# Start order, three zero fills, the order of attention and the last addition in a kernel for adaLN, infini-attention and a SwiGLU FFN

## The chip, the cores and the metric

The kernel runs on one core of one Trainium2 chip. Its time is the device time of one execution in microseconds (us). The core's engines work side by side and each takes its instructions in order from its own queue: TensorE (PE; its weight loads are listed apart as PEld), VectorE (DVE), ScalarE (ACT), GpSimd (POOL), and SyncE (SP), whose queue issues most DMA transfers. Where an engine needs what another has made, its instruction waits on a semaphore, and all that stands behind it on that engine waits with it.

## The reference, cut to what matters

```python
def _A_ref(x, wq, wk, wv, wo, beta):            # S=2048, D=576, H=32, Dh=18, N=4 segments of L=512
    ...
    g = _sigmoid(beta).reshape(1, H, 1, 1)
    for s in range(N):
        qs, ks, vs = q[:, :, s], k[:, :, s], v[:, :, s]
        logits = jnp.einsum("bhqd,bhkd->bhqk", qs, ks) * scale + mask
        p = _softmax(logits, axis=-1)
        a_dot = jnp.einsum("bhqk,bhkd->bhqd", p, vs)
        pq = phi(qs)                              # t + 1 where t > 0, exp(t) elsewhere
        num = jnp.einsum("bhld,bhde->bhle", pq, M)
        den = jnp.einsum("bhld,bhd->bhl", pq, z)[..., None] + 1e-6
        o = g * (num / den) + (1.0 - g) * a_dot
        outs.append(o)
        pk = phi(ks)
        M = M + jnp.einsum("bhld,bhle->bhde", pk, vs)
        z = z + jnp.einsum("bhld->bhd", pk)
    ...
    return o @ wo

def _B_ref(x, w_gate, w_up, w_down):             # F=4608
    return (_silu(x @ w_gate) * (x @ w_up)) @ w_down

mod = (_silu(c) @ w_mod).reshape(c.shape[0], 6, 1, -1)
sa, ca, ga, sb, cb, gb = (mod[:, i] for i in range(6))
h = _layernorm(x, axis=-1) * (1 + ca) + sa
x = x + ga * _A_ref(h, wq, wk, wv, wo, beta)
h = _layernorm(x, axis=-1) * (1 + cb) + sb
x = x + gb * _B_ref(h, w_gate, w_up, w_down)
```

All data is float32. `mask` is -1e9 for keys behind the query and zero for the keys up to it. Scale and shift of each layernorm come out of a small product of `silu(c)` with `w_mod`.

## The kernel before, in words

Tokens lie on the 128 partitions in tiles of 128 (four rows of tiles, 0 to 3, make one segment), or are transposed on TensorE so that channels lie there, in groups of 128 channels called `kt` (the fifth has 64). Products that need float32 accuracy are made from pairs of `fp32r` numbers: a value is cast to a high part (`hh`, `wqkh`, `wvh`) and DVE subtracts that from the value for the low part (`hl`, `wqkl`, `wvl`); three products of such parts make one.

**Start (0 to 18 us of the profile).** SP loads `x[0]` in two halves and a part of `w_mod` in four pieces (`wm`). DVE makes statistics of each of the four rows of tiles (lines L263 to L265; the power -1/2 is on POOL, L266), and ACT normalises them (L438, with `nb` from L437). PE multiplies `wm` by the broadcast `sgb` (the silu of `c`) into `pr`, one group of products for each piece of channels `k` in the order 4, 0, 1, 2, 3 (L449); ACT copies `pr` to `row` (L459), adding one to the scale's half by `pbias` (two fills on POOL, L456 and L457); PE turns `row` into columns (`pcr`, L463), and DVE copies them to `colv`. The transposes of the normalised `x[0]` (`pt`, L276) are issued by `transpose_group` from a later function, `heads`, and the scheduler places them among the products of `pr`; a fourth one of each group is held behind the last product (`low["pr"]`). Transposes into `fill` (L454, L465) compute nothing that is used.

**Projections (18 to 235 us).** Evacuation of the transposes by ACT (`hh`, L283) and DVE (`hl`, L285), products with the q and k weights (`pp`, L554) and with the v weights (`pv`, L583), and the memory of each segment. The statistics of the segments behind the first are made for four rows at once: one power of 128x4 on POOL (L266), then four normalisations on DVE (L270).

**Attention (235 to 527 us).** The units `u` are pairs of a segment and four heads, 32 in all (`NU`). What is issued when is written out by hand in `ORDER`, one string for each unit. Of its tokens, `s` makes scores again for the exponential on ACT, `r` makes scores for the row maximum on DVE (of unit u+2; two adjacent ones of `s` and `r` share TensorE), `V` multiplies by v, `E` ends a unit's sums, `m` and `n` prepare the maximum, `c` and `d` are the two halves of combining a unit's attention with its memory part, `M` and `X` are the wo product, `y<n>` is a part of preparing the FFN's input, `U` loads a unit, and `<` and `>` shift a token to the unit before or after. `d` is `comb_b`: DVE makes reciprocals (L774) and multiplies (`tmp`, L781), and the product is added to the output tile `o` (L782), on POOL for all units but the last, whose addition is on DVE.

Three tiles `qe0` to `qe2` need zeros outside of what is loaded into them. `early()` fills them on POOL (L342, 128x1024 each) as soon as POOL comes to them.

**Behind attention.** PE transposes `o` of the last segment (`pto`, L819, and `ptr`, L802), multiplies by wo (530.7 to 550 us), and from 550 us on the FFN runs, in which each product of 2x2 blocks is made of seven block products; the sums of blocks of its input that this needs are made before (`ys` and others, L1209 and L1221 on POOL).

The order of instructions on each engine is that of the program's text, except that a scheduler moves instructions by its own estimates of when they can run; `tc.issue_after` holds an instruction behind another, and inside `tc.manual_schedule()` the text's order stands.

Of the kernel before, what the change touches and what calls it, by code (L numbers as in the profile page):

```python
# [7 lines left out]
F32 = mybir.dt.float32  # L8
# [91 lines left out]
def f32(ap):  # L100
    return ap.bitcast(F32)
# [3 lines left out]
def block(ctx: ExitStack, tc: tile.TileContext, x, wqk, wv, wo, beta, wgu, wd, c, w_mod, wm01, out):  # L105
# [136 lines left out]
    def p1_unit(u, b, ps, tag, bufs, jp, jb, load_e):  # L242
# [9 lines left out]
        for i in range(6 - 3 * u):  # L252
            yield
        mt_a(u, ps, tag, bufs)
        mt_b(u)

    def ln_stats(wk, xs, n):
        st = wk.tile([P, n, 2, 6], F32, tag=f"st{n}", name="st")
        mv = wk.tile([P, n, 2], F32, tag=f"mv{n}", name="mv")
# [1616 lines left out]
```

## Time and profile before

| | us |
|---|---|
| median of 3 runs (1815.52 to 1815.91) | 1815.66 |
| the profiled execution | 1815.06 |
| its span | 1813.3 |
| first product of `hh` with weights (`pp`) begins | 17.91 |
| first `pto` of the last segment's last columns begins | 530.72 |

The span goes from the first to the last instruction that the profile shows; the execution's time has 1.8 us around it. In the profile a row of a timeline names start, duration, engine, line, operation, output <- inputs and shape (several equal ones in a row are put together, with their count behind an x), and in brackets for how long the engine had been idle and which instruction released it. A row of waits names the waiting instruction and the one that released it, with total, times and the longest. A duration runs from an instruction's start to its end, with all that holds it up in between.

### The profile page before, as it was taken

The numbers are of one execution on the slowest core, as the hardware profiler recorded it, in microseconds if no ns is written. First come the engines' busy times: TensorE is split into PE (matmuls) and PEld (weight loads), VectorE is DVE, ScalarE is ACT, GpSimd is POOL, SyncE is SP. The second block draws the span as 40 slices with busy tenths as digits, with TensorE's granted clock in tenths as the row PEclk, the third lists the DMA queues.
The fourth block names the chain that finished last, engine by engine and source line by source line (L and its number), as shares of the span: only waits on it lengthen the run. The fifth ranks groups of instructions, "written<-read, shape, count | busy, mean of one in ns | idle before, by whom it ended". The sixth has DMA issues, their size and how long they took to land.

```text
span 1813.3 us, 31111 instructions
## 1 busy us (share of the span) xinstructions
PE 1789.0 (99%) x11061; PEld 1515.2 (84%) x11061; DVE 1480.0 (82%) x3277; ACT 949.5 (52%) x2073; POOL 490.9 (27%) x707
## 2 busy tenths in 40 slices
PE   8999999999989999999999999999999999999999
PEld 5888867767778888888888888888888888888888
DVE  7567589999968888889888898668888888888886
ACT  6444578778866445444544444434544544544542
POOL 3000146555660544544454444100000000000000
PEclk9999999999999999999999999999999999999999
DMA  8678766577678455555544543594324324323331
GB/s 287 234 239 281 236 195 180 165 195 214 179 238 269 160 185 175 164 172 188 190 144 140 174 155 121 193 293 138 107 79 130 107 80 130 107 81 129 107 103 53
DMA packets 178563, 304.51 MB, mean 168 GB/s; under 512 B 25304, under 2 KB 108184, under 8 KB 176616
## 3 DMA queue, kind: packets, MB, share of 16 engines
q1 hardware_dynamic: 151032, 248.66, 43.9%
q10 hardware_dynamic: 27376, 53.86, 8.5%
q8 instruction: 88, 1.44, 0.3%
q14 instruction: 67, 0.55, 0.1%
HBM read 188.42 MB, written 113.33 MB: 166 GB/s over the span
## 4 chain that ended last, share of the span: by engine, by line
PE 68%; DVE 2%; DMA 1%; POOL 1%; issue 1%; ACT 1%; ACTq 0%; DVEq 0%
PE A L1388 24%; PE pd L1516 13%; PE C L1388 12%; PE pd L1497 10%; PE B L1388 6%; PE pw L846 1%; DMA y<-yD 1%; DVE wr L1338 0%; DVE wl L1353 0%; DVE dl L1378 0%; PE pt L1288 0%; ACT Pt L725 0%; PE av L744 0%; POOL Pt L730 0%; DVE acc L1526 0%
## 5 line engine op out<-in xcount | busy, mean ns | idle before, releaser
L1388 PE MATMUL A<-y,wh 128*128 128x512 f32 x1152 | 406.1, 393 | 1.2 <-ACT B L1434 0.9
L1388 PEld LDWEIGHTS A<-y,wh 128*128 128x128 f32 x1152 | 216.6, 188 | 46.2 <-ACT B L1434 2.4
L1353 DVE TENSOR_TENSOR wl<-O,wh 128x256 fp32r<-128x256 f32 x504 | 248.0, 497 | 2.1 <-ACT wh L1352 1.6
L211 DVE CUSTOM_DVE_ANT_0 junk<-s,tri 128x384 bf16<-128x384 f32 (+3 forms) x512 | 218.6, 486 | 25.2 <-PE s L689 12.7
L1388 PE MATMUL A<-y,wl 128*128 128x512 f32 x576 | 226.9, 394 | 0.0
L1502 DVE TENSOR_TENSOR acc<-acc,pd 128x576 f32<-128x576 f32 x216 | 162.4, 752 | 59.0 <-PE pd L1497 51.5
L1388 PE MATMUL C<-y,wh 128*128 128x512 f32 x576 | 203.0, 393 | 0.5 <-DVE cu L1411 0.5
L1352 ACT CAST wh<-O 128x256 fp32r<-128x256 f32 x504 | 197.6, 405 | 1.5 <-DMA yD<-st 1.2
L1526 DVE TENSOR_TENSOR acc<-acc,pd 128x576 f32<-128x576 f32 x156 | 116.9, 750 | 89.7 <-PE pd L1516 89.3
L1516 PE MATMUL pd<-dh,ah 128*128 128x288 f32 x640 | 189.0, 295 | 0.5 <-DVE x L1520 0.5
L1516 PE MATMUL pd<-dh,al 128*128 128x288 f32 x640 | 189.1, 296 | 0.0
L1516 PE MATMUL pd<-dl,ah 128*128 128x288 f32 x640 | 188.8, 295 | 0.0
L1343 POOL TENSOR_TENSOR O<-O 128x384 f32<-128x384 f32 x132 | 149.1, 1144 | 139.0 <-DMA O<-in_wgu_dram 64.3
L1457 ACT CAST ah<-sg 128x512 fp32r<-128x512 f32 x192 | 119.2, 621 | 77.9 <-DVE sg L1412 71.4
L725 ACT ACTIVATE Pt<-s 128x512 f32<-128x512 f32 x256 | 136.0, 599 | 21.4 <-PE s L718 15.2
L1458 DVE TENSOR_TENSOR al<-sg,ah 128x512 fp32r<-128x512 f32 x192 | 136.4, 710 | 10.4 <-ACT ah L1457 10.2
L1497 PE MATMUL pd<-dh,ah 128*128 128x288 f32 x448 | 133.0, 297 | 0.0
L1497 PE MATMUL pd<-dh,al 128*128 128x288 f32 x448 | 132.5, 296 | 0.0
L1497 PE MATMUL pd<-dl,ah 128*128 128x288 f32 x448 | 132.3, 295 | 0.0
L1516 PEld LDWEIGHTS pd<-dl,ah 128*128 128x128 f32 x640 | 120.5, 188 | 7.2
L1516 PEld LDWEIGHTS pd<-dh,ah 128*128 128x128 f32 x640 | 120.8, 189 | 6.8 <-DVE x L1520 0.8
L1388 PEld LDWEIGHTS C<-y,wh 128*128 128x128 f32 x576 | 108.3, 188 | 21.5 <-DVE cu L1411 1.2
(412 smaller groups left out, 4336.6 us busy)
## 6 DMA issues: line engine op xcount, KB each, us to landing
O<-in_wgu_dram SPq DMA_DIRECT2D x36, 768.0 KB
O<-oD SPq DMA_DIRECT2D x36, 512.0 KB
oD<-O ACTq DMA_DIRECT2D x34, 512.0 KB
ks<-kD SPq DMA_DIRECT2D x64, 216.0 KB
qs<-qD SPq DMA_DIRECT2D x64, 216.0 KB
O<-in_wgu_dram SPq DMA_DIRECT2D x36, 384.0 KB
rD<-wr ACTq DMA_DIRECT2D x36, 336.0 KB
wr<-rD SPq DMA_DIRECT2D x35, 336.0 KB
```

Source lines behind the costliest of these rows:

```text
L211: nc.vector.tensor_tensor_reduce(junk[:, :n], bank[:, o:o + n], tri[:, L - n:], 1.0, -3e38, op0=ALU.add, op1=ALU.max, accum_out=mcol[u][0] ...
L725: nc.scalar.activation(pt[:, h], bank, AF.Exp, scale=SCALE)
L1343: eng.tensor_tensor(o[:, d], o[:, a], o[:, b], op=op)
L1352: nc.scalar.copy(wh, o)
L1353: later.append(lambda: nc.vector.tensor_tensor(wl, o, f32(wh), op=ALU.subtract))
L1388: nc.tensor.matmul(bank, lhsT=a, rhs=b, start=(first and n == 0), stop=(n == 6), skip_group_check=not first)
L1457: nc.scalar.copy(ah, src)
L1458: later.append(lambda: nc.vector.tensor_tensor(al, src, f32(ah), op=ALU.subtract))
L1497: nc.tensor.matmul(pd[:, i, :288], lhsT=a[:, tk], rhs=w, start=(k == 0), stop=(k == 2))
L1502: nc.vector.tensor_tensor(o, o, pd[:, :, :288], op=ALU.add)
L1516: nc.tensor.matmul(pd[:, i, :288], lhsT=a[:, tk], rhs=w, start=(k == 0), stop=(k == 5))
L1526: nc.vector.tensor_tensor(o, o, pd[:, :, :288], op=ALU.add)
```

## The change

It has four parts.

1. *Start.* The block is put under `tc.manual_schedule()`. `norm0` makes the statistics of two rows and then their `nb` and normalisation, first for rows 0 and 1, then for 2 and 3; the `sgb` copy stands ahead of both. The transposes of `kt` 0 to 3 are taken out of `heads` and put among the products of `pr` by hand (`tr0`, `pt0`); eight for rows 0 and 1 ahead of the products `k` = 1 and `k` = 2, the other eight behind the last product. The five `fill` transposes ahead of `row` go, and of the nine behind it six stay. `pbias` is filled behind the statistics.
2. *Zero fills.* The three fills of `qe` are held behind the power of the second statistics (`low["ln", 4]`, the first that is made for four rows).
3. *Order.* `ORDER` has new strings with the same tokens for the same units. Two lines of 33 are shown below.
4. *Additions.* The last unit's addition is shared: DVE adds the first three of four blocks of 72 columns, POOL the fourth, and `tmp` lies in a buffer of its own (`woraw`, not in use any more). The addition of unit 29 (`NU - 3`) goes from POOL to DVE.

```diff
-    "s s n s s V0123 <<d y75 y87 E y109 y105 y44 s s y122 y98 s s y111 y76 y129 >p s s",
-    "s s s M0 y99 M1 M2 M3 y100 X <<c >M0 y116 x y124 >M1 >M2 y117 y102 y89 >M3 >X <<d <c y112 y130 y53 s y131 s s s y113 s s s y115 y127 y128 V0123 E >V0123 >E <d y125 c d y118 >c y126 >d",
+    "s T y99 y116 s s y122 y127 s >M0 <<d >M1 y86 >M2 E y129 >M3 <c <d s >X y88 y53 y100 s s s s s",
+    "s s s y123 >M0 y110 y87 y117 >M1 >M2 y76 >M3 <c y118 s s y130 s y124 >X s s s y131 s y115 V0123 y111 y89 y128 <d E >V0123 c y112 y125 >E d >c y113 y126 >d",
...
-        nc.gpsimd.tensor_tensor(rs, rs, mhalf[:, :n], op=ALU.pow)
+        low.setdefault(("ln", n), nc.gpsimd.tensor_tensor(rs, rs, mhalf[:, :n], op=ALU.pow))
...
-                nc.gpsimd.memset(f32(q_[n]), 0.0)
+                with tc.issue_after(low["ln", 4].ins):
+                    nc.gpsimd.memset(f32(q_[n]), 0.0)
...
+            man.enter_context(tc.manual_schedule())
...
-            for i in range(4):
-                mv, rs = ln_stats(wk, [xs[0][:, i, :]], 1)
-                nb = wk.tile([P, 1], F32, tag="nb1", name="nb")
-                nc.vector.tensor_scalar(nb, mv[:, 0, 0:1], rs[:, 0:1], -1.0, op0=ALU.mult, op1=ALU.mult)
-                nc.scalar.activation(xs[0][:, i, :], xs[0][:, i, :], AF.Identity, scale=rs[:, 0:1], bias=nb[:, 0:1])
+            def norm0(ids):
+                ln = [ln_stats(wk, [xs[0][:, i, :]], 1) for i in ids]
+                for i, (mv, rs) in zip(ids, ln):
+                    nb = wk.tile([P, 1], F32, tag="nb1", name="nb")
+                    nc.vector.tensor_scalar(nb, mv[:, 0, 0:1], rs[:, 0:1], -1.0, op0=ALU.mult, op1=ALU.mult)
+                    nc.scalar.activation(xs[0][:, i, :], xs[0][:, i, :], AF.Identity, scale=rs[:, 0:1], bias=nb[:, 0:1])
 
             sgb = wk.tile([P, 5, 32], F32, tag="sgb", name="sgb", bufs=1)
             nc.vector.tensor_copy(sgb, sg.unsqueeze(2).to_broadcast([P, 5, 32]))
+            norm0((0, 1))
+            norm0((2, 3))
             pr = ps.tile([P, L], F32, tag="m", name="pr", bufs=1)
+            pt0 = [ps.tile([P, L], F32, tag="s1" if kt in (2, 3) else "t", name="pt", bufs=2) for kt in range(4)]
+
+            def tr0(ks, ids):
+                for kt in ks:
+                    for i in ids:
+                        nc.tensor.transpose(pt0[kt][:, 128 * i:128 * i + 128], xs[0][:, i, 128 * kt:128 * kt + 128], ident)
...
             for k in (4, 0, 1, 2, 3):
+                if k == 1:
+                    tr0((0, 1), (0, 1))
+                elif k == 2:
+                    tr0((2, 3), (0, 1))
...
-            for i in range(5):
-                nc.tensor.transpose(fill[:, i % 4, :], wm[:, 7, 112 * i:112 * i + 128], ident)
...
+            tr0((0, 1, 2), (2, 3))
...
-            for i in range(9):
+            tr0((3,), (2, 3))
+            for i in range(6):
...
-            tmp = wk.tile([P, 320], F32, tag="tmp", name="tmp")[:, :288].rearrange("p (i h z) -> p i h z", i=4, h=4)
+            last = u == NU - 1
+            tmp = (wk.tile([P, D], F32, tag="woraw", name="tmp", bufs=1) if last else
+                   wk.tile([P, 320], F32, tag="tmp", name="tmp"))[:, :288].rearrange("p (i h z) -> p i h z", i=4, h=4)
             nc.vector.tensor_tensor(tmp, v[:, :, :, :DH], rb, op=ALU.mult)
-            (nc.vector if u == NU - 1 else nc.gpsimd).tensor_tensor(dst, dst, tmp, op=ALU.add)
+            k = 3 if last else 4 if u == NU - 3 else 0
+            if k:
+                nc.vector.tensor_tensor(dst[:, :k], dst[:, :k], tmp[:, :k], op=ALU.add)
+            if k < 4:
+                nc.gpsimd.tensor_tensor(dst[:, k:], dst[:, k:], tmp[:, k:], op=ALU.add)
```

How the instructions stand at three places (engine queues in the order in which they are issued; in brackets whom a row waits for, a name with DMAHW being a transfer).

TensorE at the start, before: the groups of `pr` and, between them, transposes of the normalised `x[0]`.

```order
L449 MATMUL pr<-wm,sgb 32x320 [waits DMAHW4_49]
L449 MATMUL pr<-wm,sgb 32x320 x3
L276 MATMUL pt<-ident,x_265 128x128 [waits DMAHW1_49,Activation_49]
L276 MATMUL pt<-ident,x_265 128x128 x3
L276 MATMUL pt<-ident,x_265 128x128 [waits Activation_49]
L276 MATMUL pt<-ident,x_265 128x128 x2
L449 MATMUL pr<-wm,sgb 32x320 [waits DMAHW5_49]
L449 MATMUL pr<-wm,sgb 32x320 x3
L276 MATMUL pt<-ident,x_265 128x128 [waits DMAHW3_49,Activation_49]
L276 MATMUL pt<-ident,x_265 128x128 x4
L449 MATMUL pr<-wm,sgb 32x320 [waits DMAHW6_49]
```

The same place in the changed kernel, where L468 is the product of `pr` and L455 the transpose:

```order
L455 MATMUL pt<-ident,x_267 128x128 x2
L468 MATMUL pr<-wm,sgb 32x320 [waits DMAHW4_49]
L468 MATMUL pr<-wm,sgb 32x320 x3
L455 MATMUL pt<-ident,x_267 128x128 x4
L468 MATMUL pr<-wm,sgb 32x320 [waits DMAHW5_49]
L468 MATMUL pr<-wm,sgb 32x320 x3
L468 MATMUL pr<-wm,sgb 32x320 [waits DMAHW6_49]
L468 MATMUL pr<-wm,sgb 32x320 x3
L455 MATMUL pt<-ident,x_267 128x128 [waits DMAHW3_49,Activation_49]
L455 MATMUL pt<-ident,x_267 128x128 [waits Activation_49]
L455 MATMUL pt<-ident,x_267 128x128 x4
```

The transposes of rows 2 and 3 (the wait for DMAHW3) have moved from between the last two groups of `pr` to behind the last.

POOL between the first and the second statistics, before; `pk` and `vs` are small fills, `omc` a copy, and L266 is the power:

```order
L266 TENSOR_TENSOR rs<-rs,mhalf 128x1 [waits DVE_49] x2
L472 MEMSET pk 128x4x64 [waits DMAHW5_49,DMAHW4_49,DMAHW6_49,DMAHW2_49,PE_49]
L342 MEMSET qe 128x1024 x3
L601 COPY omc<-omg 18x8 [waits DVE_49]
L601 COPY omc<-omg 18x8 [waits Pool_49]
L601 COPY omc<-omg 18x8 x2
L266 TENSOR_TENSOR rs<-rs,mhalf 128x4 [waits DVE_49,Pool_49]
L578 MEMSET vs_2095 128x4x32 [waits DMAHW5_49,PE_49,Activation_49]
```

And in the changed kernel, with the power at L268 and the fills at L344:

```order
L491 MEMSET pk 128x4x64 [waits DMAHW4_49,DMAHW5_49,DMAHW2_49,DMAHW6_49,PE_49,Pool_49]
L623 COPY omc<-omg 18x8 [waits DVE_49]
L623 COPY omc<-omg 18x8 [waits Pool_49]
L623 COPY omc<-omg 18x8 x2
L268 TENSOR_TENSOR rs<-rs,mhalf 128x4 [waits DVE_49,Pool_49]
L344 MEMSET qe 128x1024 x3
L600 MEMSET vs_2090 128x4x32 [waits DMAHW5_49,PE_49,Activation_49]
```

The three fills have moved from ahead of the copies to directly behind the 128x4 power. On DVE the four normalisations that wait for this power are followed by `fl` and `wvl`, as before.

POOL at the end of attention, before; L1209 and L1221 are sums for the FFN's input, L782 the additions to `o`, L730 masks:

```order
L782 TENSOR_TENSOR o_6413<-o_6413,tmp 128x4x72 [waits DVE_49]
L730 AFFINE_SELECT Pt<-Pt 128x4x128 [waits Activation_49] x2
L730 AFFINE_SELECT Pt<-Pt 128x4x128
L730 AFFINE_SELECT Pt<-Pt 128x4x128 [waits Activation_49]
L1209 TENSOR_TENSOR yh_5571<-yh_5571,yh_5573 128x256
L1209 TENSOR_TENSOR yh_5571<-yh_5571 96x256
L1209 TENSOR_TENSOR yh_5571<-yh_5571,yh_5574 96x256 [waits Pool_49]
L782 TENSOR_TENSOR o_6413<-o_6413,tmp 128x4x72 [waits DVE_49] x2
L1221 TENSOR_TENSOR ys<-yh_5571,yh_5572 128x512 [waits PE_49]
L1221 TENSOR_TENSOR o_6413<-yh_5571,yh_5573 128x512
```

And in the changed kernel (L752 masks, L1237 and L1249 sums, L810 additions):

```order
L752 AFFINE_SELECT Pt<-Pt 128x4x128
L752 AFFINE_SELECT Pt<-Pt 128x4x128 [waits Activation_49]
L1237 TENSOR_TENSOR yh_5619<-yh_5619,yh_5621 128x256 [waits Pool_49]
L1237 TENSOR_TENSOR yh_5619<-yh_5619,yh_5622 96x256 x2
L810 TENSOR_TENSOR o_6396<-o_6396,tmp 128x4x72 [waits DVE_49]
L810 TENSOR_TENSOR o_6396<-o_6396,tmp 128x72 [waits DVE_49]
L1249 TENSOR_TENSOR ys<-yh_5619,yh_5620 128x512 [waits PE_49]
L1249 TENSOR_TENSOR o_6396<-yh_5619,yh_5621 128x512
```

Behind the last masks two full additions have become one, and the last unit's 72 columns stand directly ahead of the first L1249.

DVE at the same place, before: reciprocals (L774), multiplications (L781) and the last addition (L782), for the units 29, 30 and 31.

```order
L774 RECIPROCAL r_8393<-px 128x16 [waits PE_49]
L781 TENSOR_TENSOR tmp<-px,r_8393 128x288 [waits DVE_49]
L1119 TENSOR_TENSOR yo<-yh_5574,yo 32x256 [waits DMAHW7_49,Activation_49]
L774 RECIPROCAL r_8404<-px 128x16 [waits PE_49]
L781 TENSOR_TENSOR tmp<-px,r_8404 128x288 [waits DVE_49,Pool_49]
L774 RECIPROCAL r_8416<-px 128x16 [waits PE_49]
L781 TENSOR_TENSOR tmp<-px,r_8416 128x288 [waits DVE_49,Pool_49]
L782 TENSOR_TENSOR o_6413<-o_6413,tmp 128x4x72 [waits DVE_49]
```

And in the changed kernel (L796, L805, L808):

```order
L796 RECIPROCAL r_8366<-px 128x16 [waits PE_49]
L805 TENSOR_TENSOR tmp<-px,r_8366 128x288 [waits DVE_49,Pool_49]
L808 TENSOR_TENSOR o_6396<-o_6396,tmp 128x4x72 [waits DVE_49]
L1145 TENSOR_TENSOR yo<-yh_5621,yo 128x256 [waits Activation_49]
L1147 TENSOR_TENSOR yo<-yh_5622,yo 32x256 [waits DMAHW0_49]
L796 RECIPROCAL r_8399<-px 128x16 [waits PE_49]
L805 TENSOR_TENSOR tmp<-px,r_8399 128x288 [waits DVE_49]
L796 RECIPROCAL r_8411<-px 128x16 [waits PE_49]
L805 TENSOR_TENSOR tmp<-px,r_8411 128x288 [waits DMAHW6_49,DVE_49]
L808 TENSOR_TENSOR o_6396<-o_6396,tmp 128x3x72 [waits DVE_49]
```

Unit 29's addition stands on DVE behind its multiplication, and the last unit's multiplication no longer waits for POOL.

More of the change, by code (lines that the diff above doesn't have):

```diff
@@ L255, in p1_unit @@
         mt_b(u)
+    low = {}
     def ln_stats(wk, xs, n):
@@ L270, in xhat, with transpose_group @@
         nc.vector.tensor_scalar(dst, src, mv[:, i, 0:1], rs[:, i:i + 1], op0=ALU.subtract, op1=ALU.mult)
-    def transpose_group(pt, src, kt, behind=None):
+    def transpose_group(pt, src, kt):
         n = P if kt < 4 else 64
         for i in range(4):
-            with tc.issue_after(behind.ins) if behind and i == 3 else ExitStack():
-                nc.tensor.transpose(pt[:n, 128 * i:128 * i + 128], src(i)[:, 128 * kt:128 * kt + n], ident)
+            nc.tensor.transpose(pt[:n, 128 * i:128 * i + 128], src(i)[:, 128 * kt:128 * kt + n], ident)
     def evac_split(wk, pt, kt, hi, lo, sc, bi, tag="hf"):
@@ L377, in load_x @@
                 yield
-        rq, low = {}, {}
+        rq = {}
         def load_qk(t):
@@ L422, in block @@
             m0 = pool(p0, "m0")
+            man = ExitStack()
+            man.enter_context(tc.manual_schedule())
             gx = load_x(0)
@@ L451, in block @@
             low["pr"] = last
-            fill = ps.tile([P, 4, P], F32, tag="p", name="fill", bufs=3)
-            for i in range(5):
-                nc.tensor.transpose(fill[:, i % 4, :], wm[:, 7, 112 * i:112 * i + 128], ident)
             pbias = wk.tile([P, 1], F32, tag="pbias", name="pbias", bufs=1)
@@ L468, in block @@
             nc.vector.tensor_copy(colv[0:64, 4], pcv[0:64, 1, 2, :, 0])
+            man.close()
         pb = pool(p1, "pb", 2)
@@ L507, in trans_in @@
             for kt in range(5):
-                pt = ps.tile([P, L], F32, tag="s1" if s == 0 and kt in (2, 3) else "t", name="pt", bufs=2)
-                transpose_group(pt, lambda i: xs[s][:, i, :], kt, low["pr"] if s == 0 else None)
+                if s == 0 and kt < 4:
+                    pt = pt0[kt]
+                else:
+                    pt = ps.tile([P, L], F32, tag="t", name="pt", bufs=2)
+                    transpose_group(pt, lambda i: xs[s][:, i, :], kt)
                 if kt < 4:
```

1 line of the change is left out of this document (added), and 54 rows, old and new, of the table ORDER.

## The prediction

> **What bounds the kernel now.** I read the page first, then busy time by stage, then PE's waits, then the timeline at the places the diff touches. The page's busy time:
>
> ```profile
> span 1813.3 us, 31111 instructions
> PE 1789.0 (99%) x11061; PEld 1515.2 (84%) x11061; DVE 1480.0 (82%) x3277; ACT 949.5 (52%) x2073; POOL 490.9 (27%) x707
> ```
>
> PE is idle for only 24.3 us in all, so an edit can gain little unless it touches that idle time or the clock. By stage (start:end, length, then busy time and instructions of PE, PEld, DVE, ACT and POOL, then granted clock, DMA share, GB/s):
>
> ```profile
> 0.00:17.91 17.91, 9.95 (x73) 5.12 (x73) 7.69 (x30) 6.20 (x9) 10.10 (x35) 1.00 0.83 306
> 24.00:50.00 26.00, 25.87 (x124) 21.07 (x123) 22.28 (x46) 17.75 (x34) 2.66 (x5) 1.00 0.94 315
> 250.00:514.00 264.00, 260.60 (x2506) 187.27 (x2503) 240.26 (x1028) 207.45 (x427) 156.30 (x335) 1.00 0.65 186
> 529.00:560.00 31.00, 29.28 (x173) 27.26 (x174) 23.36 (x44) 17.19 (x37) 6.58 (x7) 0.89 0.99 332
> ```
>
> The first row is the start (8.0 us of PE idle). In the second PE has no slack, so a shift of the start is carried on whole. The third is steady attention: PE idle 3.4 us, DVE idle 23.7. The fourth has the clock at 0.89. PE's waits (total, times, longest) name the two single stalls:
>
> ```profile
> PE pr L449 <- DVE mv L264: 7.6, 1, 7.6
> PE pto L819 <- DVE o L782: 3.3, 1, 3.3
> ```
>
> The first is the wait for the first data; the second is the addition that the change shares out.
>
> **Term 1: the start.** The rows (start, duration, engine, line, operation; in brackets the idle time before it and its releaser):
>
> ```profile
> 8.95 1.54 DVE L263 BATCH_NORM_STATS2 st<-x 128x6 f32<-128x288 f32 x4 [1.29 <-DMA x<-in_x_dram]
> 10.41 0.32 DVE L437 TENSOR_SCALAR nb<-mv,rs 128x1 f32<-128x1 f32 x2
> ...
> 10.64 1.62 ACT L438 ACTIVATE x<-x,nb,rs 128x576 f32<-128x576 f32 x2 [7.97 <-DVE nb L437]
> 11.70 1.76 PE L276 MATMUL pt<-ident,x 128*128 128x128 f32 x7
> ...
> 13.39 0.89 PE L449 MATMUL pr<-wm,sgb 128*32 128x320 f32 x8
> 14.15 0.49 DVE L388 CAST wqkh<-wraw 128x640 fp32r<-128x640 f32 x1 [0.63 <-DMA wraw<-in_wqk_dram]
> 14.21 0.76 PE L276 MATMUL pt<-ident,x 128*128 128x128 f32 x5
> 14.90 0.75 PE L449 MATMUL pr<-wm,sgb 128*32 128x320 f32 x8
> 16.66 3.43 POOL L342 MEMSET qe<- 128x1024 f32 x3
> 17.03 2.17 DVE L388 CAST wqkh<-wraw 128x640 fp32r<-128x640 f32 x2
> 19.12 1.54 DVE L389 TENSOR_TENSOR wqkl<-wraw,wqkh 128x640 fp32r<-128x640 f32 x2
> 21.32 0.50 PE L554 MATMUL pp<-hl,wqkh 128*128 128x512 f32 x1
> ```
>
> Before, nb of rows 0 and 1 stood behind the four statistics of rows 2 and 3, which waited for their data until 8.95. Now it stands ahead of them, so both rows are normalised 1.5 us sooner or more (8.95 against 10.41) and their transposes leave the path. The five transposes (0.76) ahead of the last weight group go behind it: the column vector and the first casts come 0.8 us sooner, perhaps 1.2 with the gaps between. The two casts took 2.17 while the zero fills ran, against 0.49 for the one without: 2.17 - 2*0.49 = 1.2 more goes with the fills. In all 2.0 to 2.4 for DVE's chain of casts, differences and hl; I take 1.8, as ACT's hh and the third piece of weights can limit it too: **-1.8**, bounds -0.7 (the transposes alone) and -2.4. The sgb copy ahead of the statistics costs nothing: PE waits for weights there. The bias fills, now behind a pair of small powers on POOL, are needed only by the row. The fill transposes (14 before, 6 now) stood in PE's idle time and cost nothing.
>
> **Term 2: the fills at the second statistics.** The three fills now stand on POOL directly behind this power, and four DVE normalisations wait for the same power:
>
> ```profile
> 48.04 1.02 POOL L266 TENSOR_TENSOR rs<-rs,mhalf 128x4 f32<-128x4 f32 x1 [18.78 <-DVE rs L265]
> 49.09 2.05 DVE L270 TENSOR_SCALAR x<-x,mv,rs 128x576 f32<-128x576 f32 x4 [1.20 <-POOL rs L266]
> ...
> 51.66 0.75 DVE L112 TENSOR_TENSOR wvl<-wvraw,wvh 128x576 fp32r<-128x576 f32 x1
> 53.13 0.29 PE L583 MATMUL pv<-wvl,hr 128*128 128x288 f32 x1
> 17.88 1.32 DVE L388 CAST wqkh<-wraw 128x640 fp32r<-128x640 f32 x1
> ```
>
> The last row is the second cast under the fills: 1.32 - 0.49 = 0.83 of waiting behind one fill. A normalisation has the same form (one float32 SBUF input, 0.51 each), and the fills follow without a wait, so each of the three goes ahead of one: 3*0.83 = 2.5 late. Behind them on DVE stands wvl, which is done at 52.41 and read at 53.13, 0.72 before PE needs it; PE's queue is in order. The stall is 2.5 - 0.7 = **+1.8**. Bounds: 0 (the normalisations go first) and 3.43 - 0.72 = 2.7. DVE's own lag vanishes in later idle time, PE's doesn't. So terms 1 and 2 about cancel.
>
> **Term 3: the last addition.**
>
> ```profile
> 525.66 0.26 DVE L774 RECIPROCAL r<-px 128x16 f32<-128x16 f32 x1 [3.24 <-PE px L766]
> 526.28 1.54 POOL L782 TENSOR_TENSOR o<-o,tmp 128x288 f32<-128x288 f32 x2
> 527.10 0.46 DVE L781 TENSOR_TENSOR tmp<-px,r 128x288 f32<-128x288 f32 x1 [0.30 <-POOL o L782]
> 527.59 2.98 DVE L782 TENSOR_TENSOR o<-o,tmp 128x288 f32<-128x288 f32 x1
> 527.78 1.26 POOL L1221 TENSOR_TENSOR ys<-yh,yh 128x512 f32<-128x512 f32 x1
> 529.00 1.26 POOL L1221 TENSOR_TENSOR o<-yh,yh 128x512 f32<-128x512 f32 x1
> 530.72 0.45 PE L819 MATMUL pto<-ident,o 128*128 128x128 f32 x1 [3.27 <-DVE o L782]
> ```
>
> The DVE add of 288 columns is shown with 2.98, where the multiplication of 288 took 0.46. It ends at 530.57, just after POOL's second L1221 (530.26): it waited for both. Now tmp has its own buffer (no 0.30 wait: it ends at 527.26), unit 29's addition is off POOL, and DVE adds 216 columns (0.46*216/288 = 0.35) while POOL's 72 columns (at most a quarter to a half of 0.77, say 0.4) stand ahead of L1221. One after the other they end at 528.0; PE resumes at about 528.1 for 530.72. I take **-2.5**. If DVE's part loses the port to one L1221 it is -2.5 + 1.26 = -1.3, to both about -0.1; the best is -3.0 (both side by side). Unit 29's addition on DVE costs nothing: DVE idles 3.24 before 525.66; without that cover 0.4.
>
> The Trainium skill, "SBUF — State Buffer", section "SBUF: two separate sides", says that between a DVE operation with two SBUF inputs and a GpSimd one that reads SBUF, whichever starts first holds the shared port pair for its whole instruction, and the other fully blocks. By that rule the add would have waited for one operation at most. The 2.98 disagrees, so the measurement decides; by the rule term 3 is what I take, by the row it can still be lost to both.
>
> **Term 4: the clock.** Windows of 3.41 us, same columns:
>
> ```profile
> 518.92:522.33 3.41, 2.84 (x30) 1.38 (x32) 3.25 (x8) 2.84 (x7) 2.26 (x4) 1.00 0.66 222
> ...
> 525.74:529.16 3.42, 1.20 (x7) 0.78 (x7) 2.93 (x5) 0.05 (x1) 3.42 (x5) 1.00 0.95 319
> 529.16:532.57 3.41, 1.85 (x10) 1.74 (x10) 2.10 (x2) 1.10 (x2) 3.41 (x3) 0.50 1.01 405
> 532.57:535.98 3.41, 3.41 (x16) 3.41 (x15) 1.38 (x2) 1.69 (x4) 3.01 (x4) 0.50 1.02 339
> ```
>
> After a window with PE busy 1.20 of 3.42 the clock is halved for two windows; after one with 2.84 it isn't. PE works from 530.72 to 535.98 at half speed, 5.3 us, which costs half: 2.6. With the stall at 0.7 instead of 3.3, such a window holds some 2 to 2.5 us of work, nearer to 2.84 than to 1.20, so I take **-2.6**; the other end is 0.
>
> The Trainium skill, "TensorE: Matmul & The Clock Gate", Part 1, gives free-running windows of about 3.4 us and a drop after an idle one. The length agrees with these rows (two windows at 0.50); the drop here came after a window that was 35% busy, so idle need not mean empty. By the page's rule a window with 2 us of work keeps the clock, and rival 2 falls away.
>
> **Term 5: the order of attention.** The tokens are the same; 252 adjacent score pairs share TensorE instead of 254. No row shows what another order does. PE's idle 3.4 us bounds the gain; the loss has no bound but DVE, whose commonest work there is the row maximum:
>
> ```profile
> L211 DVE CUSTOM_DVE_ANT_0 junk<-s,tri 128x384 bf16<-128x384 f32 (+3 forms) x512 | 218.6, 486 | 25.2 <-PE s L689 12.7
> ```
>
> One such operation (486 ns) late in each of some 30 units would be +14.6. I take 0, nearer to the small bound, since 240 of 264 us of DVE work leaves 23.7 to absorb shifts.
>
> **Sum.** -1.8 + 1.8 - 2.5 - 2.6 + 0 = -5.1. The profiled execution took 1815.06 us (1.8 around its span), 0.6 below the median 1815.66. 1815.06 - 5.1 = 1810.0; against the median **1810.6 us**. A measurement of this kernel tells 0.2% (3.6 us) from no change.
>
> **Rivals.**
> 1. *The last addition loses the port again.* For it: the 2.98. Against: fewer POOL operations ahead. Then term 3 is -0.1 and term 4 is 0: 1815.66 - 0.1 = 1815.6, no change. Lost once, with the clock falling: -1.3, 1814.4, no change.
> 2. *The clock falls all the same,* after a shorter stall. Sum -2.5: 1813.2, no change.
> 3. *Slower: attention in the new order starves DVE.* Place: the waits of the row maximum on the scores, 12.7 us now. Price 486 ns a unit, +14.6 over 30 units: 1810.6 + 14.6 = 1825.2. It decides from 5.1 + 3.6 = 8.7 us, 0.29 us a unit. For it: DVE is 91% busy there, and nearly every line is reordered. Against: the slack of 23.7.
> 4. *The new order gains too,* up to PE's 3.4 us of idle: 1807.2, and a little more where it shortens the last units' run to the addition.
>
> **Chances.** The forecast 0.45; rival 1 lost twice 0.13; lost once 0.10 (half of it with the clock kept: -1.3 - 2.6 = -3.9, faster); rival 2 0.08; rival 3 0.15; rival 4 0.09. Faster: 0.45 + 0.05 + 0.09 = 0.59. Same: 0.13 + 0.05 + 0.08 = 0.26. Slower: 0.15. The range goes from 1804.3 (rival 4 with the best ends of terms 1 to 3: 1807.2 - 0.6 - 1.8 - 0.5) to 1817.6 (rival 1 with the weak ends of terms 1 and 2: 1815.6 + 1.1 + 0.9); outside lie rival 3 and a few hundredths below.
>
> **What would show it.** Term 1: two casts at 0.49 each and hl's first product near 19.5. Term 2: fills of some 3.4 us behind the 128x4 power, four normalisations taking about 4.5 instead of 2.05, and PE waiting for wvl. Term 3: the wait of pto on o at about 0.7, and a DVE addition of 216 columns well under 1 us. Term 4: a clock of 1.00 from 529 to 536. Term 5: DVE idle in attention near 24 us. The forecast is wrong if the addition again shows some 3 us, if the clock still falls, or if attention's length moves by more than 4 us.

## The result, and the profile after

The changed kernel takes 1809.41 us (median of 8 runs, 1807.21 to 1813.06) for 1815.51 us of the kernel before beside it (8 runs, 1813.69 to 1815.91). The ratio is 0.997, with a 95% interval of 0.9960 to 0.9979: 6.1 us less by the medians. The profiled execution took 1810.5 us (4.6 less than that of before) with a span of 1808.8. Single executions of one kernel lie 2 to 4 us to either side of its median, some further, so places are compared by profiles and totals by medians; a profile shows one execution alone.

The page of the changed kernel:

```profile
span 1808.8 us, 31104 instructions
PE 1783.9 (99%) x11053; PEld 1512.5 (84%) x11053; DVE 1485.3 (82%) x3278; ACT 947.8 (52%) x2073; POOL 493.5 (27%) x707
```

PE's idle time did not shrink: 24.9 us now, 24.3 before. Its busy time fell by 5.1 us. Its waits (total, times, longest) say that the stall at the last addition is gone and that others have come:

```profile
PE pr L468 <- DVE mv L266: 7.8, 1, 7.8
PE pw L874 <- DVE xr L879: 2.4, 1, 2.4
PE C L1416 <- DVE cu L1439: 1.5, 1, 1.5
PE pv L605 <- DVE wvl L112: 1.4, 1, 1.4
PE A L1416 <- DMA y<-yD: 1.4, 1, 1.4
PE pto L847 <- DVE tmp L805: 0.9, 1, 0.9
```

The timeline of the changed kernel, first at the start and at the second statistics, then at the last addition:

```profile
16.24 0.88 DVE L390 CAST wqkh<-wraw 128x640 fp32r<-128x640 f32 x2
19.25 0.50 PE L576 MATMUL pp<-hl,wqkh 128*128 128x512 f32 x1
...
46.77 2.75 POOL L344 MEMSET qe<- 128x1024 f32 x3
46.87 4.42 DVE L272 TENSOR_SCALAR x<-x,mv,rs 128x576 f32<-128x576 f32 x4 [1.20 <-POOL rs L268]
46.87 2.96 DVE L272 TENSOR_SCALAR x<-x,mv,rs 128x576 f32<-128x576 f32 x1 [1.20 <-POOL rs L268]
...
520.59 0.66 PE L788 MATMUL px<-ident,avs 128*128 128x128 f32 x4 [0.28 <-ACT avs L779]
522.06 0.38 DVE L808 TENSOR_TENSOR o<-o,tmp 128x216 f32<-128x216 f32 x1
522.17 0.72 PE L847 MATMUL pto<-ident,o 128*128 128x128 f32 x4 [0.93 <-DVE tmp L805]
522.60 1.27 POOL L1249 TENSOR_TENSOR ys<-yh,yh 128x512 f32<-128x512 f32 x1
```

The reader is to see that the two casts take 0.88 together, that the four normalisations take 4.42 under the fills for 2.05 before, 2.96 of it in the first of them (the row with x1), which ends 0.31 behind the third fill, that the shared addition takes DVE 0.38, and that PE is idle for 0.93 ahead of the first four transposes of `o` (`pto`). Before, three of these four ran ahead of the last addition, and PE waited 3.27 for the fourth, the one that needs it. In the changed kernel this fourth one begins at 522.59, 0.42 behind the first.

From the first product by v (`av`) to the last group of `px`, which is attention, the same table as in the prediction gives for the kernel before

```profile
230.23:526.23 296.00, 291.45 (x2798) 208.51 (x2797) 262.42 (x1114) 231.16 (x475) 174.24 (x372) 1.00 0.65 185
```

and for the changed kernel

```profile
229.89:520.97 291.08, 288.42 (x2799) 207.61 (x2797) 265.35 (x1115) 229.64 (x475) 175.02 (x372) 1.00 0.65 187
```

It is 4.9 us shorter: 1.9 of this is idle time of PE, and 3.0 is busy time with the same number of products but one. The same stretch takes 290.9 to 292.7 us in all eleven profiles of this case with the new order, and 296.0 to 297.2 in the three with the old one.

Behind attention, the timeline of the changed kernel:

```profile
528.96 4.87 POOL L1371 TENSOR_TENSOR O<-O 128x384 f32<-128x384 f32 x4 [2.57 <-DMA O<-in_wgu_dram]
533.86 0.62 ACT L1365 CAST wr<-O 96x512 fp32r<-96x512 f32 x1 [4.02 <-POOL O L1371]
538.24 0.37 PE L874 MATMUL pw<-woh,hh 128*128 128x288 f32 x1 [2.40 <-DVE xr L879]
```

and rows of busy times, ahead of the wait of PE and just behind it:

```profile
529.00:532.00 3.00, 3.00 (x26) 3.00 (x25) 2.88 (x5) 0.84 (x3) 2.92 (x3) 1.00 1.05 317
532.00:536.00 4.00, 3.84 (x30) 3.61 (x28) 2.02 (x3) 2.14 (x5) 1.83 (x2) 1.00 1.01 362
538.00:542.00 4.00, 3.76 (x18) 3.79 (x19) 3.68 (x9) 2.07 (x6) 0.00 (x0) 0.63 1.01 363
```

POOL waits 2.57 for the load of O; ACT waits 4.02 for POOL with a cast of `wr` that stands ahead of the `hh` cast of the last rows; PE waits 2.40; and then its clock is lower for a while (0.63 on average from 538 to 542). In the profile of before none of these waits is there; POOL came to O without one:

```profile
531.66 4.00 POOL L1343 TENSOR_TENSOR O<-O 128x384 f32<-128x384 f32 x4
```

Where the lead over the kernel before stood, in the two profiles:

| place | before | after | lead |
|---|---|---|---|
| first product of `hl` | 21.32 | 19.25 | 2.1 |
| `pv` that waits for `wvl` | 53.13 | 52.62 | 0.5 |
| last group of `px` | 525.85 | 520.59 | 5.3 |
| the `pto` that needs the last addition | 530.72 | 522.59 | 8.1 |
| the 50th `pw` of the wo product behind it | 541.10 | 530.59 | 10.5 |
| first `A` of the FFN | 550.0 | 543.6 | 6.4 |
| first `pd` | 580.7 | 575.3 | 5.4 |
| last `pd` group | 1809.5 | 1805.0 | 4.5 |

So the lead rises to 10.5 us in the wo product, where the full clock has added 2.4 to the 8.1, and more than half of it is given back, at the entry to the FFN and in the FFN. One figure tells most of what follows: from the last `px` product to the first `pd`, the kernel before takes 580.7 - 526.2 = 54.5 us and the changed one 575.3 - 521.0 = 54.3, though the addition's stall and the halved clock of before lie between these two.

### The profile page after: what moved, and what is told of

The parts are those of the page before. It is cut to its first block, busy times and chain, and to the rows that moved or that the text cites. A ratio compares the mean times of both kernels' runs of the same rounds, so it can differ in the third digit from the quotient of the medians.

```text
span 1808.8 us, 31104 instructions
## 1 busy us (share of the span) xinstructions
PE 1783.9 (99%) x11053; PEld 1512.5 (84%) x11053; DVE 1485.3 (82%) x3278; ACT 947.8 (52%) x2073; POOL 493.5 (27%) x707
## 4 chain that ended last, share of the span: by engine, by line
PE 78%; DMA 3%; DVE 3%; POOL 1%; issue 1%; ACT 1%; ACTq 0%; SPq 0%; POOLq 0%; DVEq 0%
PE A L1416 24%; PE pd L1544 14%; PE C L1416 12%; PE pd L1525 10%; PE B L1416 6%; PE av L766 3%; PE pw L874 2%; PE s L711 2%; PE s L740 2%; PE pn L1010 1%; DMA y<-yD 1%; DVE junk L211 1%; DMA O<-in_wgu_dram 1%; DMA xD<-xr 1%; PE pw L951 1%
```

## The experiments

Each was timed beside the kernel before, whose medians were 1815.0 to 1816.2.

### The new order alone

```diff
 (the kernel before)
-ORDER = (... old strings ...)
+ORDER = (... new strings ...)
```

> The kernel before with the new order of attention and nothing else changed. Theory: the order itself makes attention shorter, as it did between 250 us and the last products by v in the changed kernel (from 0.34 to 5.26 us ahead), so here the last px begins some 4.5 to 5 us sooner than 526.2; the last addition, still whole and on DVE, again makes PE wait about 3 us and the clock falls, and the end comes 4 to 5 us sooner: about 1811. Rival: the lead in attention came from the start and the additions (their phase against DVE and POOL); then the new order alone gives less than 1.5 us and the time stays above 1814.

Measured: 1811.57 us, ratio 0.9983 (0.9973 to 0.9993), 3.9 us less than before by the medians. In its profile `av` runs from 229.9 to 519.9, against 230.2 to 524.8 before, so the shorter attention belongs to the order itself. What in the order makes it shorter, no run here shows. The last addition, the same as before, is again:

```profile
522.98 2.98 DVE L782 TENSOR_TENSOR o<-o,tmp 128x288 f32<-128x288 f32 x1
```

The rival (less than 1.5 us, above 1814) is out by the median and by the profile; the weak end of the interval alone, 1.3 us, would leave it room.

### The additions alone

```diff
 (the kernel before, with the new comb_b)
+k = 3 if last else 4 if u == NU - 3 else 0
...
```

> The kernel before with only the additions of the last unit and of unit 29 changed. Theory: PE's wait for the last addition falls from 3.3 to under 1 us and the clock stays full, 4.5 to 5.5 us ahead at the wo product; the transfers behind attention give some of it back, so 1811 to 1813 in all. Rival: the last DVE addition loses its access to the L1221 sums again, since it is the old order that sets when these come; then the wait stays near 3 us and the time near 1815.

Measured: 1813.31 us, ratio 0.9991 (0.9981 to 1.0001): 2.2 us less by the medians, 0.3 above the range that was expected, and just inside what can't be told from no change. The mechanism is there in the profile:

```profile
527.18 0.38 DVE L786 TENSOR_TENSOR o<-o,tmp 128x216 f32<-128x216 f32 x1
...
527.71 0.30 PE L825 MATMUL pto<-ident,o 128*128 128x128 f32 x1 [1.02 <-DVE o L786]
```

The wait is 1.02 for 3.27, so the old order of POOL's sums did not cost the port. From the last `px` (526.1) to the first `pd` (576.3) it takes 50.2 us, 4.3 less than before: most of terms 3 and 4 (5.1) comes out in this profile. The medians show 2.2; the execution profiled (1811.2) was 2.1 faster than the median of its kernel.

### The start and the fills alone

```diff
 (the changed kernel, with ORDER and comb_b of before)
```

> The changed kernel with the old order of attention and the old last addition: only the start and the moved fills are left. Theory: hl's first product comes about 1.9 us sooner than in the kernels with the old start, the normalisations under the fills give some 1.5 back at 53 us, and what is left ends at the wait for x of a later segment near 148 us, as in the changed kernel: no measurable difference, 1814.9 to 1815.6. Rival: the start's gain is carried to the end, 1813.5.

Measured: 1814.72 us, ratio 0.9997 (0.9988 to 1.0006): no difference, as expected. The first product of `hl` began at 18.8, and PE waited 1.6 for `wvl`.

The three parts alone give 3.9, 2.2 and 0.6 us by the medians, 6.7 together; the whole change gives 6.1. The intervals are too wide (some 2 us each) to read a loss from that.

### The fills at another place

```diff
 (the changed kernel)
-with tc.issue_after(low["ln", 4].ins):
+with tc.issue_after(low["omc"].ins):      # the last of the omc copies
     nc.gpsimd.memset(f32(q_[n]), 0.0)
```

> The changed kernel with the three zero fills behind the omc copies (25.8 to 27.6 us) instead of behind the second statistics' power. Theory: four normalisations take about 2.05 instead of 4.42, PE does not wait for wvl (1.4), and the lead against the kernel before stays at 2.1 us from 53 us on instead of 0.4. The end gains less than that: if the transfers behind attention bound the entry to the FFN, it lies within 0.5 us of the changed kernel (1809.4); if nothing absorbs it, 1.6 less (1807.8).

Measured: 1809.41 us, ratio 0.9967 (0.9955 to 0.9978): the changed kernel's time. Fills and normalisations no longer meet:

```profile
27.25 2.75 POOL L344 MEMSET qe<- 128x1024 f32 x3
...
45.76 2.05 DVE L272 TENSOR_SCALAR x<-x,mv,rs 128x576 f32<-128x576 f32 x4 [1.14 <-POOL rs L268]
```

so term 2 is shown: its 2.4 us on DVE are the fills'. That the end gains nothing has earlier causes than the entry to the FFN: against the changed kernel's profile, the lead of 2.1 us that this one has at 140 us shrinks to 1.1 at the place shown below, and the rest is lost near 400 us, inside attention. At 146 us DVE's statistics wait for the data of the last segment, the sums `macc` of the modulation stand behind them, and PE waits for these, in this kernel for 1.48:

```profile
145.31 1.18 DVE L265 BATCH_NORM_STATS2 st<-x 128x6 f32<-128x288 f32 x3 [1.05 <-DMA x<-in_x_dram]
...
147.69 0.61 PE L407 MATMUL pc<-ones,macc 128*128 128x1 f32 x4 [1.48 <-DVE macc L400]
```

In the changed kernel's first profile this PE wait is 0.44, in its second (below) 1.26. An earlier start alone does not set it: with work added (below) `hl` began late, at 19.5, and the wait was 2.18.

### One cast on ACT behind another

```diff
 (the changed kernel)
-WW = (11, 15, 18, 22, 27)
+WW = (11, 16, 18, 22, 27)
```

> The changed kernel with the second wr cast and the wh cast beside it on ACT issued one step later, behind the hh cast of the last rows. Theory: PE's 2.4 us wait in the wo product came from ACT's queue, where these casts waited 4.0 us for POOL's sums of O ahead of hh; without it the wait goes, the clock stays full from 536 to 543 (1.6 more), and 2 to 4 us are gained, less what the FFN's first products then wait for y: 1806 to 1808. Rival: the transfers themselves are late and the wait only moves to y or O: within 0.7 us of 1809.4.

Measured: 1810.55 us (12 runs), ratio 0.9972 (0.9963 to 0.9981), 1.1 us above the changed kernel's median: the gain of 2 to 4 us did not come. The profile speaks for the theory nonetheless: PE's wait for `xr` fell from 2.4 to 0.5, and from the last `px` (524.6) to the first `pd` (576.0) it takes 51.4 us for 54.3, with waits of 1.0 and 0.8 for `y` and `cu` still in it. But this execution had lost 2.8 us against the changed kernel's near 148 us, where PE waited 1.69 and then ran for a time at a lower clock (0.59 from 152 to 155). So the edit shortens this stretch, and a gain in time is not shown.

### More work on PE behind attention, twice

```diff
 (the changed kernel, wo_r)
-for kt in range(4):
+for kt in list(range(4)) * (7 if (s, i) == (3, 0) else 1):
     nc.tensor.transpose(pt[:, kt, :], ot[s][:, i, 128 * kt:128 * kt + 128], ident)
```

> The changed kernel with 24 more transposes of the finished output (their result is overwritten) ahead of the wo product of the last segment: some 3 us of work put on TensorE just behind the last addition. Theory: the entry to the FFN is bound by the transfers (xr, O and y) that start when attention ends, so a lead of PE beyond some 5 us is lost there; of the 3 us no more than 0.7 reach the FFN's first pd and the end: 1809.5 to 1810.5, with PE's waits in the wo product and for y shorter by as much. Rival: PE's own work is the path; then the time is 3 us longer, about 1812.5.

Measured: 1813.17 us (12 runs), ratio 0.9983 (0.9972 to 0.9994), 3.8 us more than the changed kernel: my expectation (0.7 at most) failed. Since single executions of the changed kernel spread, both were run again on one chip.

> The changed kernel once more, beside the next two on the same chip, since its single executions lie between 1807.2 and 1813.1. Theory: about 1809.5, and a part of the executions loses one to three us before attention, where PE waits for the sums of the modulation near 148 us (0.4 in the first profile, 1.7 and 2.2 in two others) and the clock falls when that wait is long. Rival: the spread comes from the entry to the FFN, and the wait near 148 us is the same in a second profile.

> The 24 added transposes once more, beside the changed kernel on the same chip. Theory after the first run (3.8 us longer by the medians, against 0.7 at most that I expected): TensorE's work reaches the end nearly whole, 2 to 4 us longer than the changed kernel of this call. Rival: the first difference came from executions with a long wait near 148 us, which has nothing to do with the added work; then the medians of this call differ by less than 1.5 us.

Measured: 1810.17 us (5 runs) for the changed kernel and 1812.77 us (11 runs) with the added work, 2.6 us more. In this second pair of profiles PE's wait of 2.7 in the wo product fell to 0.2 under the added work, and the FFN's first `pd` came at 576.5 for 576.1: from the last `px` to the first `pd` it takes 54.2 us for 54.4. There the work is hidden, as expected. Yet the last `pd` group comes at 1806.8 for 1804.6. The other 1.8 us appear inside the FFN, and what makes them is open. The spread of the changed kernel is not settled either: its wait near 148 us is 0.44 in one profile and 1.26 in the other, and the clock fell behind it in neither; another 0.9 us between the two appear near 400 us, in attention. The wait of 2.7 in this second profile, unlike that of 2.40 in the first, left the clock at 1.00.

### The last addition whole on DVE

```diff
 (the changed kernel)
-k = 3 if last else 4 if u == NU - 3 else 0
+k = 4 if last or u == NU - 3 else 0
```

> The changed kernel with the last unit's addition not shared: all 288 columns on DVE, tmp still in its own buffer. Theory: a DVE addition of two SBUF inputs that starts while POOL adds loses to the next two POOL sums as well, as it did before (2.98): about 2.9 again, PE's wait some 2.5 longer than now (3.4 for 0.9), and the time within 1.5 us of the changed kernel since the transfers hide most of it. Rival: the own buffer and the shorter run of POOL additions were enough, and it takes 0.5 to 1.4: PE waits less than 2.

Measured: 1809.19 us, ratio 0.9961 (0.9949 to 0.9974), the changed kernel's time. The addition takes half of what it took before:

```profile
521.98 0.79 POOL L810 TENSOR_TENSOR o<-o,tmp 128x288 f32<-128x288 f32 x1
522.73 1.26 POOL L1249 TENSOR_TENSOR ys<-yh,yh 128x512 f32<-128x512 f32 x1
...
522.86 1.45 DVE L808 TENSOR_TENSOR o<-o,tmp 128x288 f32<-128x288 f32 x1
```

It begins at 522.86, behind POOL's addition (ended 522.77) and just behind the start of the first L1249 (522.73), waits for that one alone, and ends at 524.31. PE waits 1.0 for it, behind the 0.9 for `tmp`. So it is neither the theory (2.9) nor quite the rival (up to 1.4): with its own buffer and one addition fewer on POOL it is held by one sum in place of two, and with the sharing by none.

### The last segment's x in one transfer, and the loads behind attention sooner

The first adds to the two edits above (fills behind `omc`, cast behind) a third:

```diff
 (load_x; fills behind omc, WW with 16)
+w = 4 if s == 3 else 2
-for i in range(0, 4, 2):
-    nc.sync.dma_start(t[:, i:i + 2, :], x[s][:, i:i + 2, :])
+for i in range(0, 4, w):
+    nc.sync.dma_start(t[:, i:i + w, :], x[s][:, i:i + w, :])
```

> The changed kernel with three edits: fills behind the omc copies, the second wr cast on ACT behind the hh cast of the last rows, and the rows of the last segment's x loaded by one transfer instead of two, the second of which stood on SP behind two stores. Theory: the statistics at 146 us no longer wait for x (1.3 us) nor PE for macc, so the start's lead of 2.1 to 2.5 us stays to attention, which carries it; the end gains 1 to 2 us: 1807.5 to 1808.5. Rival: the entry to the FFN absorbs this as well, or the larger transfer delays others: 1809 to 1810.

Measured: 1807.56 us, ratio 0.9959 (0.9947 to 0.9971). PE does not wait for `macc` any more, and the first `A` of the FFN is 10.9 us ahead of before; then PE waits longer for the FFN's input:

```profile
PE C L1417 <- DMA y<-yD: 2.4, 1, 2.4
```

Why are these loads late? The queue of SP in the changed kernel, as a timeline and then a row of its waits:

```profile
519.11 0.36 SPq L1151 DMA_DIRECT2D yD<-yo  x1
...
520.34 1.39 SPq L841 DMA_DIRECT2D xr<-in_x_dram  x3
521.84 0.36 SPq L1349 DMA_DIRECT2D O<-in_wgu_dram  x1
```

```profile
SPq L1151 <- DVE yo L1145: 6.9, 1, 6.9
```

SP stood 6.9 us in front of a store of the FFN's input, with the loads of `xr`, O and `y` behind it. Before, the first of these `xr` loads was issued at 523.23, 2.6 us ahead of the last group of `px` (525.85); in the changed kernel it is 0.25 ahead of it (520.59). The order made attention shorter (5.3 us at the last `px`) by more than it moved its last store (2.7, from 522.68 to 519.98). The fourth edit issues the last two stores from ACT:

```diff
+yeng[0] = nc.scalar if tok in ("y113", "y126") else nc.sync
 parts[int(tok[1:])]()
...
-nc.sync.dma_start(yD[0][o][:, kb:kb + 3:2, c], f32(st))
+yeng[0].dma_start(yD[0][o][:, kb:kb + 3:2, c], f32(st))
```

> The kernel with three edits, and the last two stores of the FFN's input (which SP waited 6.9 us for, ahead of the loads of xr, O and y) issued by ACT instead. Theory: the xr loads start some 6 us sooner, O lands up to 2 us sooner (8.6 us behind the first xr load so far), POOL's wait for O and PE's waits for y and in the wo product shrink together by 1 to 2 us, and the end comes at 1805.5 to 1807. Rival: O and y wait for memory that attention frees, not for the queue; then only xr comes sooner, and the time stays at 1807 to 1808.

Measured: 1805.34 us (5 runs, 1803.87 to 1807.19), ratio 0.9943 (0.9931 to 0.9955), 4 to 5 us below the changed kernel and the fastest of all. The loads now begin as follows:

```profile
510.45 1.38 SPq L842 DMA_DIRECT2D xr<-in_x_dram  x3
518.20 0.33 SPq L1351 DMA_DIRECT2D O<-in_wgu_dram  x1
```

The expectation had the gain in POOL's wait for O, and it isn't there. SP now waits 6.2 us for PE's `av` ahead of the O load, which is issued 1.1 ahead of the last `px` (0.9 behind it with three edits): the store had held it back by 2 us, and now attention holds it, as the rival said. And POOL waits for the store itself, ahead of sums of O that begin no sooner behind the last `px` than with three edits (8.8 us, for 7.5):

```profile
526.46 1.65 POOL L1251 TENSOR_TENSOR ys<-yh,yh 96x512 f32<-96x512 f32 x1 [3.03 <-DMA yD<-yo]
528.07 4.88 POOL L1373 TENSOR_TENSOR O<-O 128x384 f32<-128x384 f32 x4
```

What falls away is PE's 2.4 for `y` and the lower clock behind it (0.57 from 546 to 550 with three edits, 1.00 now): the last of these `y` loads is issued 9.9 us behind the last `px` for 13.1. From the last `px` (519.3) to the first `pd` (569.8) it takes 50.5 us, for 53.4 with three edits. The lead over before, 10.9 us there, loses 3 us half way through the FFN, where PE waits 2.1 for the second half's `y`.

### The old addition with the four edits

```diff
 (the kernel with four edits, with comb_b of before)
```

> The kernel with four edits, and the additions of units 29 and 31 put back as they were before. Theory: with the loads behind attention issued sooner, the entry to the FFN no longer hides a late PE, so PE's 3 us wait for the last addition and the 2 to 2.6 us of halved clock come back whole: 4.5 to 5.5 us longer than with four edits (1805.3), about 1810. Rival: the transfers still bound the entry, and the addition is worth no more than the 2.2 us by which the medians differ when it is changed alone in the kernel before: 1807.5 or less.

Measured: 1809.51 us, ratio 0.9972 (0.9961 to 0.9982), 4.2 us more than with four edits. The first `pd` is at 574.3 for 569.8, 4.5 us, and the addition shows 2.98 once more:

```profile
520.88 2.98 DVE L805 TENSOR_TENSOR o<-o,tmp 128x288 f32<-128x288 f32 x1
```

From the last `px` (519.4) to the first `pd` it takes 54.9 us, 4.4 more than with the new addition. The theory holds, a little under its lower end. Taken together, from the last `px` to the first `pd`:

| | old addition | new addition |
|---|---|---|
| old order | 54.5 (before) | 50.2 |
| new order | 54.8 (with the old start) | 54.3 and 54.4 (the change, two profiles) |
| new order and four edits | 54.9 | 50.5 |

In these profiles the addition and its clock are worth 4.3 us in the old order and 4.4 with four edits, and some 0.4 in the new order alone, where the loads come late. In the medians only the third row is as clear: 4.2, with intervals that don't overlap. They show 2.2 in the old order, and 2.2 between the new order alone and the whole change, 0.6 of it the start's by its own run; these intervals reach some 2 us to either side, so the small worth in the changed kernel rests on the profiles.

## Why the prediction was right or wrong

The total was forecast at 1810.6 and came out at 1809.4, within the range and with the sign that was given 0.59. That it is so near is luck in part: terms 1 to 4 came to 5.6 us in the profile (forecast 5.1), but the sum has nothing for the 4.9 gained in attention and nothing for the 6 lost behind it (from a lead of 10.5 to 4.5), and these two cancel. By a sign that the prediction itself names, attention's length moving by more than 4 us, its account was wrong there.

- **Term 1, the start (-1.8):** right in size. The casts take 0.88, and `hl`'s first product came at 21.3, 20.5 and 20.5 in the three profiles with the old start, and between 18.5 and 19.5 in the eleven with the new one, 1.8 sooner on average. The sentence that such a shift is carried on whole holds only to the end of its row, 50 us: the wait for x at 146 us takes more of it (1.0 of 2.1 with the fills elsewhere).
- **Term 2, the fills (+1.8):** right in size, not in its path. The normalisations were 2.4 late (2.5 in the working), PE waited 1.4 for `wvl`, and the lead fell by 1.6. With the fills elsewhere all of this is gone. But the working had each of the three fills go ahead of one normalisation; the first one waited for all three (2.96, where it takes 0.51 alone), and the others took 0.56 to 0.57 each.
- **Term 3, the last addition (-2.5):** right in mechanism, a little too small in size. The lead grew by 2.9, from 5.3 to 8.1, just short of my best end of 3.0: DVE's 216 columns took 0.38 beside POOL's 72 (0.53), where the sum had the two one after the other.
- **Term 4, the clock (-2.6):** right where it was looked for, since the clock is 1.00 from 529 to 536; it brought the lead from 8.1 to 10.5, so 2.4. But behind a new stall of 2.40 it fell a few microseconds later, and 1.5 of the lead went from there to the first `A`. In the changed kernel's second profile it did not fall, behind a stall of 2.7.
- **Term 5, the order (0):** wrong; it was -4.9 in the profile and 3.9 of the 6.1 us by the medians. Two steps failed. I took 0 between two bounds because no row showed what the order does. And the bound of the gain, PE's 3.4 us of idle time between 250 and 514, was no bound: 3.0 of the 4.9 came out of PE's busy time. The score products `s` make up most of it: from the start of each to the start of PE's next product takes 104.7 us in all before and 100.5 after; 1.5 of these 4.2 is idle time. Products overlap in the profile (those of 128x288 begin 0.13 apart and are shown with 0.29), so a short wait between two can show as busy time; whether it is that, or that adjacent score products share TensorE in another way, is open.
- **What was left out:** the entry to the FFN. Terms 3 and 4 were worked out as if PE alone set the end of that stage, though its row showed a DMA share of 0.99. The loads that feed it did not move with attention; they stood behind a store on SP. Of the lead of 10.5, 2.5 went in PE's wait in the wo product, 1.5 under the lower clock, 1.0 up to the first `pd`, where PE waits 1.5 for `cu` instead of 0.5, and 0.9 in the FFN. The table of the old and the new addition shows the loss in single profiles, and the 4.2 us of the old addition among four edits in the medians too; the runs with work added to PE agree only as far as the first `pd`.

Of the rivals, the port (1) did not come about in the change, and its whole size is seen wherever the old addition stands. The clock (2) fell, but later, and in one of two profiles. The slower attention (3) did not occur. The fourth, that the order gains too, was given 0.09 and is what happened, with more than its bound.

The sentence on the Trainium skill ("SBUF — State Buffer", section "SBUF: two separate sides": one operation holds the port, the other side blocks for that one) has both outcomes here. The whole addition that began behind a POOL operation's start waited for just that one (1.45). The four that stood waiting while POOL went from its addition to the next sum let that sum and the one behind it go first (2.98 each), which the rule as I read it doesn't give.

## What to carry to other kernels

The idle time of the engine that looks full does not bound what a new order can gain: here 3.0 of 4.9 us came out of its busy time. Before a stall is priced at its full length, look up which transfers the next stage needs, from which queue they are issued, and what stands ahead of them there; here a store on SP ahead of the loads, and a cast on ACT that waited for them ahead of one that PE needed, cost most of what a faster addition was worth, as far as the profiles of this stretch show it: with the cast moved alone it took 51.4 us instead of 54.3, and the moved store brought it from 53.4 to 50.5. And where several early gains each meet a wait for a transfer, lift that wait first.

## What the runs showed of the hardware that was not expected

- A DVE operation can lose to several POOL operations in a row. An addition that was already waiting when POOL went on to its next operation lost to the next two: 2.98 in the kernel before, with the new start alone, with the new order alone and with the old addition among four edits, each ending about 0.3 us behind the second of POOL's sums. The first normalisation behind the second statistics lost to all three zero fills: 2.96, ending 0.31 behind the third. At the start of the kernel before, by contrast, two casts and the fills took turns: the casts took 0.93 and 1.32, and the second and third fill 1.30 and 1.29 for 0.96. What decides between the two is open.
- One and the same program's executions differ by several microseconds (1807.2 to 1813.1), and two profiles of it show a wait near 148 us of 0.44 and 1.26. Where such a wait was long (1.69 and 2.18), the clock fell behind it (0.59 and 0.50 from 152 to 155) and 2.8 and 4.7 us were lost there against the changed kernel's first profile, in runs whose edits stand behind attention.
